# Group 1's coarse scores from unpooled q, a mask made later, and a replanned order

## The chip, the cores and the metric

The kernel runs on one core of a Trainium2 chip. The metric is device time in microseconds, the median over runs. The core has five engines with a queue each: TensorE (PE in the profile, its weight loads PEld), VectorE (DVE), ScalarE (ACT), GpSimd (POOL) and SyncE (SP), which here issues every DMA. An engine runs its instructions in the order in which they were written; engines wait for each other by semaphores.

## The reference, cut to what matters

Two attentions are added, and the sum goes through a dense layer pair. B = 8, H = 8, S = 576, D = 64; the dense part has 4608 tokens, width 512, inner width 2048.

```python
q_d = q.reshape(B, H, Sd, factor, D).mean(axis=3)      # factor 4, Sd = 144; k_d, v_d alike
out_d = sm_attn(q_d, k_d, v_d)                          # softmax attention, coarse
out_up = np.repeat(out_d, factor, axis=2)
mask = np.abs(pos[:, None] - pos[None, :]) < factor     # a band of 7
scores = np.where(mask, scale * np.matmul(q, k.transpose(0, 1, 3, 2)), -1000000000.0)
...
out_local = np.matmul(attn, v)
x = (out_up + out_local)        # to [B * S, H * D]
h = x @ w_in
g = h - np.tanh(h)
return (g @ w_out)
```

## The kernel before, in words

**Units.** Two heads of one batch make a pair p (0 to 31), two pairs a group n (0 to 15), four pairs a batch. A group's q and k (i = 0 for q, i = 1 for k) come in as fp32 tiles `qkn`; each of a group's pairs has an index y (0, 1).

**One group's preparation.** `reorder` (L480) casts to bf16 into `qr`. `turn` (L496) transposes with nine TensorE matmuls into a PSUM bank (L520), copies out to `qk` (L529, whole or a half per y), and pools by four with two adds: `half` (L533) and `qkd` (L538). Tables say which engine may do each of these: `RE` and `RS` for the cast (whole or halves), `TU` and `TS` for the copy, `AD` and `AS` for the adds. A table entry may leave the choice to the planner. `prep_v` casts v to `vw` (L443, table `CV`); `pool_v` pools v on TensorE with a constant (L462, L464) and copies it out to `vd` (L469, table `VD`).

**One pair's attention.** `s1` makes four of five blocks of the band's scores (L587); ACT takes the exponential (L623). `s2` makes the fifth block and the coarse scores (L606): for each half i of the pooled keys and each head hh one matmul of the pooled k with the pooled q, 144 columns wide; ACT takes two more exponentials (L649, L652). For the first four pairs the band's bias is added on TensorE (L581); for later ones DVE multiplies the exponentials by a 0/1 `mask` (L627, L656). `outs` multiplies with v (L669, L675); DVE takes the reciprocal of the sums (L686) and normalises into `ln` (L688). The result goes back into `xT`: for pairs in the table `UP` by matmuls that also repeat the coarse rows (L723, L728) and a copy on ACT or DVE (L734); else by transposes (L744 to L748) and an addition on DVE (L753); from pair 12 on by a DMA transpose and additions (L708).

**Banks.** Two PSUM banks `ps_ts` and two `ps_ox` serve all pairs; the first four have a second set, `ps_ts1` and `ps_ox1`, which is given to the dense part afterwards. Pairs that share a bank follow one another through it.

**Dense.** `mm1` (L777) makes 512 tokens by 128 inner columns, ACT takes the tanh (L786), DVE the difference into `gT` (L789); `mm2` (L832) makes the output, ACT copies it (L843), SP stores it. Block 0 needs the first batch's `xT`, that is pairs 0 to 3; block 1 needs pairs 4 to 7 too.

**Order.** Every piece of work is recorded with an engine (or alternatives), an assumed duration in ns, the keys it reads and writes, and a priority (10 per pair, 20 per group; lower is earlier). `Program.order` (L71) is a list scheduler: each engine takes the ready piece of the lowest priority at the planned time, with a fixed latency between engines (L25) and a margin `spare` (L254) which depends on the priority. The instructions are written out in the planned order, so the assumed durations set the order and not the time on the chip. `URG` raises the priority of chosen pieces (-2 is ahead of the dense part's -1); `LATE` sets the priority of a pair's output, normalisation and way back; `PLACE` and `PV` set where turns and pooled v stand among the pairs. Where the plan leaves TensorE idle early on, filler matmuls (L1064) are written.

**Constants.** POOL makes the identity, the group pattern, the bias, the repeating pattern `spread` (L313) and the mask (L317), which at L936 needs the bias alone and has priority 38.

Of the kernel before, what the change touches and what calls it, by code (L numbers as in the profile page):

```python
# [163 lines left out]
def kernel(  # L164
# [16 lines left out]
    G = S // 4  # L181
# [72 lines left out]
    def spare(pri, eng, to):  # L254
        if eng == "DMA":
            return 2500 if pri >= 140 else 1500 if pri >= 80 else 0
        level = (pri >= 120) + (pri >= LATER)
        return SPARE[to == "PE"].get(eng, (0, 0, 0))[level]
    LATER = 180
    SPARE = ({"POOL": (0, 500, 1000)},  # L260
             {"POOL": (0, 1000, 1500), "DVE": (0, 300, 800), "ACT": (0, 200, 500)})
    P.spare = spare
# [233 lines left out]
    def turn(n, i):  # L496
# [47 lines left out]
        for k, (ys, yy) in enumerate(each if parted else both):  # L544
            table = (TURN_H[parted - 1][k] if parted else
                     TURN[3 if n >= FI else TU.get((n, i), 1)])
            P.choice([(eng, ns, lambda fn=fn, ys=ys: copy(fn, ys)) for eng, ns, fn in table],
                     reads=ts, writes=[("qk", s, i, y) for y in yy],
                     pri=URG.get("turn", {}).get(n, pri))
        parted = AS.get((n, i), 0)  # L550
# [13 lines left out]
    def attention(p):  # L564
# [34 lines left out]
        def s2():  # L599
            for hh in range(2):  # L600
                score(4, hh, 512 * hh, sc2)
            for i in range(2):
                for hh in range(2):
                    rows = slice(64 * hh, 64 * hh + 64)
                    c = 512 * hh + 96 + G * i
                    T.matmul(sc2[:, c:c + G], pT[rows, 1, y, 16 * i:16 * i + 128],  # L606
                             pT[rows, 0, y, :], start=True, stop=True)
# [7 lines left out]
        qkds = [("qkd", sq, i, y) for i in range(2)]  # L615
# [10 lines left out]
        if not first:  # L626
            op("DVE", 900, lambda: V.tensor_tensor(  # L627
                out=e1, in0=e1,
                in1=mask[:, 0:480].unsqueeze(1).to_broadcast([128, 2, 480]),
                op=ALU.mult), reads=["mask"], writes=[("E", se, 0)], pri=pri)  # L630
# [4 lines left out]
        if MERGE <= p < NPAIR - 1:  # L635
            ahead, more = nexts[p + 1]

            def both():
                ahead()
                s2()  # L640
            op("PE", 800, both, reads=qks + qkds + more, writes=ts + ox, pri=pri)
        else:
            op("PE", 380 * cold, s2, reads=qks + qkds, writes=ox if p >= MERGE else ts,
               pri=pri)
# [10 lines left out]
        if not first:  # L655
            op("DVE", 450, lambda: V.tensor_tensor(  # L656
                out=e2v, in0=e2v,
                in1=mask[:, 480:576].unsqueeze(1).to_broadcast([128, 2, 96]),
                op=ALU.mult), reads=["mask"], writes=[("E", se, 1)], pri=pri)
# [191 lines left out]
    def dense(kb):  # L851
# [18 lines left out]
        if kb == NBLK:  # L870
# [5 lines left out]
    P_A, LATE = 5000, {0: 25, 2: 40, 3: 40}  # L876
# [5 lines left out]
    PV = {2: 0, 3: 0, 4: -1, 5: -1, 6: 0}  # L882
    PLACE = {2: (1, 3), 3: (1, 2), 4: (4, 4), 5: (1, 2), 6: (4, 4), 7: (1, 1), 8: (3, 3)}
# [7 lines left out]
    CV = {0: 3, 1: 0, 2: 0, 3: 3, 4: 0, 5: 0, 6: 3, 7: 1, 8: 2, 9: 0, 10: 1, 11: 3}  # L891
# [4 lines left out]
    RE = {(0, 0): 0, (0, 1): 0, (1, 0): 1, (1, 1): 1, (2, 0): 1, (2, 1): 0, (3, 0): 3, (3,  # L896
          1): 0, (4, 0): 2, (4, 1): 1, (5, 0): 0, (5, 1): 0}
# [3 lines left out]
    TU = {(0, 0): 0, (0, 1): 0, (1, 0): 2, (1, 1): 2, (2, 0): 0, (2, 1): 0, (3, 0): 2, (3,  # L901
          1): 0, (4, 0): 0, (4, 1): 1, (5, 0): 1, (5, 1): 0}
    re_v, re_a, re_p = (("DVE", 480, V.tensor_copy), ("ACT", 580, A.copy),
# [6 lines left out]
    VD = {0: 1, 1: 2, 2: 1, 3: 0, 4: 1, 5: 0, 6: 1}  # L910
    RS = {(0, 1): 2, (1, 0): 4, (1, 1): 1}
    UP = {0: 0, 1: 0, 2: 0, 3: 3, 4: 3, 8: 0, 11: 3}
    UP_COPY = [("ACT", 660, A.copy), ("DVE", 720, V.tensor_copy)]
    UP_H = [[("ACT", 370, A.copy)], [("DVE", 410, V.tensor_copy)]]
    half_v, half_p = ("DVE", 420, 260, V), ("POOL", 650, 500, GP)
# [5 lines left out]
    TS = {(0, 0): 1, (0, 1): 2, (1, 1): 2, (2, 1): 2, (4, 0): 2, (5, 0): 2, (5, 1): 1}  # L921
    AS = {(1, 0): 2, (1, 1): 1, (2, 0): 1, (2, 1): 1, (5, 0): 1, (5, 1): 4, (6, 1): 1}
    URG = {'e1': {4: -2, 5: -2, 6: -2, 7: -2, 8: -2, 9: -2, 10: -2, 11: -2}, 'e2': {0: -2,
          1: -2, 2: -2, 3: -2, 4: -2, 5: -2, 6: -2, 7: -2, 8: -2, 9: -2, 10: -2, 11: -2},
          'norm': {0: -2, 1: -2, 2: -2, 3: -2, 4: -2, 5: -2, 6: -2, 7: -2}, 'add': {0: -2,
          1: -2}, 'turn': {4: -2, 5: -2}, 'vd': {4: -2, 5: -2}}
    ADDERS = [[("DVE", 760, 440, V), ("POOL", 1190, 850, GP)],
              [("POOL", 1190, 880, GP)], [("DVE", 760, 440, V)]]
    AD = {(0, 0): 1, (0, 1): 0, (1, 0): 0, (1, 1): 1, (2, 0): 1, (2, 1): 0, (3, 0): 0, (3,
          1): 1, (4, 0): 0, (4, 1): 0, (5, 0): 0, (5, 1): 2}  # L930
# [28 lines left out]
    for p in range(NP):  # L959
        load_v(p)  # L960
    stages = []
# [134 lines left out]
```

The softmax here doesn't subtract the row's maximum and nothing guards it: scores larger than these inputs give would overflow.

## Time and profile before

| what | value |
|---|---|
| median of 6 runs | 335.49 us (334.8 to 336.36) |
| the profiled execution, whole | 334.8 us |
| its span, first to last instruction | 333.1 us |
| granted TensorE clock | 0.999 |
| PE busy | 319.6 us (96%) |
| PEld busy | 168.6 us (51%) |
| DVE busy | 234.9 us (71%) |
| ACT busy | 209.8 us (63%) |
| POOL busy | 155.1 us (47%) |
| mm1 and mm2 matmuls recorded | 553 and 540, 512 columns each |
| first dense matmul | 28.64 us |

A share of busy time is a mean over the whole span. The kernel has a front, in which the first four pairs are made, and a long stretch after it in which dense matmuls and the other 28 pairs share TensorE. Matmuls are pipelined: a row's duration is longer than the distance to the next one, so TensorE's work is read from distances between starts and from its idle time. A few matmul records are missing from the trace.

### The profile page before, as it was taken

How to read it: one execution, taken by the hardware profiler on the slowest of the kernel's cores; microseconds unless marked ns; L12 is line 12 of the kernel's file. 1: busy time of each engine (PE TensorE's matmuls, PEld its weight loads, DVE VectorE, ACT ScalarE, POOL GpSimd, SP SyncE). 2: the span in 40 equal slices, each digit the busy share in tenths (PEclk: the TensorE clock that was granted, in tenths of full speed). 3: DMA queues.
4: the chain of work that ended last, by engine and by line, in shares of the span. 5: the costliest groups of instructions: out<-in, count | busy, mean ns of one | idle time of the engine just before them, and what ended most of it. 6: DMA issues, size and time to landing. Idle time of an engine off the chain costs nothing.

```text
span 333.1 us, 6822 instructions
## 1 busy us (share of the span) xinstructions
PE 319.6 (96%) x2563; PEld 168.6 (51%) x2606; DVE 234.9 (71%) x386; ACT 209.8 (63%) x338; POOL 155.1 (47%) x183
## 2 busy tenths in 40 slices
PE   8778999999999999999999999999999999999996
PEld 5454555655554555554445444444444444444444
DVE  3698989689989879989688878787666443344300
ACT  1775877768958587667777786986654444434411
POOL 8673776249799479794938385752000000000000
PEclk9999999999999999999999999999999999999999
DMA  6999999998973899998999899742232100100012
GB/s 215 260 389 306 324 317 311 271 281 222 319 231 82 224 191 302 194 241 226 242 249 257 223 243 232 100 104 83 60 79 69 33 31 31 63 33 31 31 70 90
DMA packets 96878, 60.47 MB, mean 182 GB/s; under 512 B 74510, under 2 KB 80078, under 8 KB 96846
## 3 DMA queue, kind: packets, MB, share of 16 engines
q1 hardware_dynamic: 96846, 60.04, 67.1%
q8 instruction: 20, 0.33, 0.4%
q14 instruction: 12, 0.10, 0.1%
HBM read 43.05 MB, written 9.44 MB: 158 GB/s over the span
## 4 chain that ended last, share of the span: by engine, by line
PE 85%; DVE 6%; POOL 3%; issue 3%; ACT 1%; POOLq 0%; DVEq 0%; ACTq 0%
PE ps_hy L777 36%; PE ps_hy L832 34%; PE ps_ts L587 3%; PE ps_ox L669 3%; PE ps_ox L675 2%; PE ps_ts L520 2%; DVE ln L688 1%; DVE qk L529 1%; PE ps_hy L807 1%; DVE half L533 1%; ACT qk L529 1%; PE ps_ox L462 1%; POOL half L533 1%; PE ps_ox L606 1%; PE ps_ox L520 1%
## 5 line engine op out<-in xcount | busy, mean ns | idle before, releaser
L777 PE MATMUL ps_hy<-xT,w_in_sb 128*128 128x512 bf16 x553 | 141.8, 379 | 2.2 <-issue 1.1
L832 PE MATMUL ps_hy<-w_out_sb,gT 128*128 128x512 bf16 x540 | 137.2, 379 | 1.4 <-issue 0.5
L789 DVE TENSOR_TENSOR gT<-ps_hy,uy 128x512 bf16<-128x512 f32 x144 | 95.3, 685 | 56.7 <-ACT uy L786 55.3
L786 ACT ACTIVATE uy<-ps_hy 128x512 f32<-128x512 f32 x144 | 83.5, 601 | 61.9 <-PE ps_hy L777 57.2
L777 PEld LDWEIGHTS <-w_in_sb 128*128 128x128 bf16 x576 | 53.1, 98 | 59.3 <-issue 1.0
L832 PEld LDWEIGHTS <-gT 128*128 128x128 bf16 x560 | 52.3, 98 | 58.1
L533 POOL TENSOR_TENSOR half<-qk 128x576 f32<-128x576 bf16 (+1 forms) x33 | 34.8, 1058 | 44.9 <-ACT qk L529 39.7
L688 DVE TENSOR_TENSOR ln<-ps_ox,r 128x896 bf16<-128x896 f32 x30 | 32.7, 1089 | 0.8
L623 ACT ACTIVATE E<-ps_ts 128x960 bf16<-128x960 f32 x30 | 29.4, 980 | 2.1 <-PE ps_ts L587 2.1
L843 ACT COPY uy<-ps_hy 128x512 f32<-128x512 f32 x35 | 20.6, 590 | 14.3 <-PE ps_hy L832 12.6
L443 POOL CAST vw<-vst 128x640 bf16<-128x640 f32 x27 | 25.5, 949 | 7.6 <-DMA vst<-in_v_dram 4.1
L708 DVE TENSOR_TENSOR xT<-lnT 128x480 bf16<-128x480 bf16 (+1 forms) x40 | 27.8, 711 | 0.0
L627 DVE TENSOR_TENSOR E<-E,mask 128x960 bf16<-128x960 bf16 x28 | 23.5, 840 | 5.5 <-ACT E L623 5.5
L356 POOL TENSOR_TENSOR qkn<-qkn 128x512 f32<-128x512 f32 (+1 forms) x18 | 25.3, 1405 | 2.5 <-ACT uy L786 1.6
L529 ACT COPY qk<-ps_ts 128x1152 bf16<-128x1152 bf16 (+1 forms) x16 | 16.1, 1005 | 16.4 <-DVE qk L529 6.3
L538 POOL TENSOR_TENSOR qkd<-half 128x288 bf16<-128x288 f32 (+1 forms) x31 | 20.4, 661 | 5.8 <-DVE half L533 4.6
L529 ACT COPY qk<-vst 128x1152 bf16<-128x1152 bf16 x10 | 22.1, 2210 | 0.9 <-POOL half L533 0.7
L669 PEld LDWEIGHTS <-E 128*128 128x128 bf16 x300 | 15.3, 98 | 7.3 <-issue 0.6
L669 PE MATMUL ps_ox<-vw,E 128*128 128x65 bf16 x300 | 18.2, 194 | 0.5 <-DVE xT L734 0.3
L587 PEld LDWEIGHTS <-qk 64*128 64x128 bf16 x320 | 9.6, 95 | 17.9 <-issue 15.6
L491 POOL CAST qr<-qkn 128x1152 bf16<-128x1152 f32 (+1 forms) x14 | 16.1, 1156 | 4.8 <-DMA qkn<-in_k_dram 4.5
L491 DVE CAST qr<-qkn 128x1152 bf16<-128x1152 f32 (+1 forms) x18 | 16.4, 913 | 2.2 <-DMA qkn<-in_q_dram 2.2
(107 smaller groups left out, 294.6 us busy)
## 6 DMA issues: line engine op xcount, KB each, us to landing
vst<-in_v_dram SPq DMA_DIRECT2D x62, 160.0 KB, 4.8
qkn<-in_q_dram SPq DMA_DIRECT2D x32, 288.0 KB, 4.2
qkn<-in_k_dram SPq DMA_DIRECT2D x32, 288.0 KB, 4.9
out_dram<-uy SPq DMA_DIRECT2D x35, 256.0 KB, 2.4
qkn<-in_v_dram SPq DMA_DIRECT2D x9, 512.0 KB, 5.2
gT<-in_moe_w_in_dram SPq DMA_DIRECT2D x4, 1024.0 KB, 9.1
xT<-in_moe_w_out_dram SPq DMA_DIRECT2D x8, 256.0 KB, 4.4
gT<-in_moe_w_out_dram SPq DMA_DIRECT2D x2, 1024.0 KB, 8.9
```

The lines of the kernel that those rows point to most:

```text
L443: P.choice([(eng, ns, lambda fn=fn: fn(out=vw[w][:, 2 * jj:2 * jj + 2, :, 0:64], in_=vst[s])) for eng, ns, fn in CAST_V[CV.get(p, 1)]], re ...
L491: P.choice([(eng, ns, lambda fn=fn, x0=x0, x1=x1: fn(out=dst[:, x0:x1], in_=srt[:, x0:x1])) for eng, ns, fn in table], reads=[("qkn", sn, ...
L529: fn(out=o[:, ys].rearrange("p y (g a) -> p y g a", a=A6), in_=b16.rearrange("p (a g y) -> p y g a", a=A6, y=2)[:, ys])
L533: eng.tensor_tensor(out=half[:, ys], in0=four[:, ys, :, 0:2], in1=four[:, ys, :, 2:4], op=ALU.add)
L623: op("ACT", 980, lambda: A.activation(out=e1, in_=ps[:, :, 0:480], func=AF.Exp, scale=SCALE), reads=ts, writes=[("E", se, 0)], pri=URG.get ...
L669: T.matmul(po[:, hh, 65 * t:65 * t + 65], E[se][:, c:c + 128], vw[w][:, 2 * jj + hh, t, :], start=True, stop=True)
L688: op("DVE", 1090, lambda: V.tensor_tensor(out=ln[sl].rearrange("p n (h d) -> p h n d", d=D), in0=blocks[:, :, :, 0:64], in1=r[s].unsqueeze ...
L708: up=up: eng.tensor_tensor(out=xo[:, QW * t0:QW * t0 + nt * n].rearrange("p (t g a) -> p t g a", t=nt, a=4), in0=lnT[sl][:, t0:t0 + nt, 0: ...
L777: T.matmul(ps_hy[slot], w_in_sb[:, dc, fc * 128:(fc + 1) * 128], xT[dc][:, kb * 512:kb * 512 + 512], start=(dc == 0), stop=(dc == N_DC - 1))
L786: op("ACT", 490, lambda: A.activation(out=u[us], in_=ps_hy[slot], func=AF.Tanh), reads=[("hy", slot)], writes=[("u", us)], pri=-1)
L789: op("DVE", 620, lambda: V.tensor_tensor(out=gT[g][:, fc, :], in0=ps_hy[slot], in1=u[us], op=ALU.subtract), reads=[("hy", slot), ("u", us) ...
L832: T.matmul(ps_hy[slot], gT[g][:, fc, ts * 128:ts * 128 + 128], w_out_sb[:, fc, :], start=(fc == 0), stop=(fc == N_FF - 1))
```

## The change

Pairs of groups in the new set `QP` (group 1 alone) take their coarse scores from the unpooled q: the four tokens of a coarse row are read from `qk` with a step of four, in four matmuls that add up in PSUM. The pooled adds of that group's q (L533, L538) are left out. The mask is recorded after the loads of v, and waits for v of pair 1. Assumed durations and tables of the planner are set anew.

```diff
         level = (pri >= 120) + (pri >= LATER)
+        if 40 <= pri < 120 and to == "PE":
+            return MID.get(eng, 0)
         return SPARE[to == "PE"].get(eng, (0, 0, 0))[level]
-    LATER = 180
+    LATER = 200
...
+    MID = {'POOL': 0, 'DVE': 0, 'ACT': 0}
...
+        if i == 0 and n in QP:
+            return
         parted = AS.get((n, i), 0)
...
                     c = 512 * hh + 96 + G * i
+                    if hb in QP:
+                        for a in range(4):
+                            T.matmul(sc2[:, c:c + G], pT[rows, 1, y, 16 * i:16 * i + 128],
+                                     qT[rows, a:576:4], start=(a == 0), stop=(a == 3))
+                        continue
                     T.matmul(sc2[:, c:c + G], pT[rows, 1, y, 16 * i:16 * i + 128],
                              pT[rows, 0, y, :], start=True, stop=True)
...
-        qkds = [("qkd", sq, i, y) for i in range(2)]
+        qkds = [("qkd", sq, i, y) for i in range(hb in QP, 2)]
...
-            op("DVE", 900, lambda: V.tensor_tensor(
+            op("DVE", 780, lambda: V.tensor_tensor(
...
-            op("PE", 380 * cold, s2, reads=qks + qkds, writes=ox if p >= MERGE else ts,
+            op("PE", (380 + 400 * (hb in QP)) * cold, s2, reads=qks + qkds, writes=ox if p >= MERGE else ts,
...
-            op("DVE", 450, lambda: V.tensor_tensor(
+            op("DVE", 600, lambda: V.tensor_tensor(
...
-    P_A, LATE = 5000, {0: 25, 2: 40, 3: 40}
+    P_A, LATE = 5000, {1: 25}
...
-    PV = {2: 0, 3: 0, 4: -1, 5: -1, 6: 0}
-    PLACE = {2: (1, 3), 3: (1, 2), 4: (4, 4), 5: (1, 2), 6: (4, 4), 7: (1, 1), 8: (3, 3)}
+    PV = {2: -1, 3: 1, 4: 0, 5: -1, 6: 0}
+    PLACE = {2: (0, 0), 3: (0, 2), 4: (4, 4), 5: (1, 4), 6: (4, 4), 7: (1, 1), 8: (1, 3)}
...
-    CV = {0: 3, 1: 0, 2: 0, 3: 3, 4: 0, 5: 0, 6: 3, 7: 1, 8: 2, 9: 0, 10: 1, 11: 3}
+    CV = {0: 3, 1: 1, 2: 2, 3: 0, 4: 3, 5: 2, 6: 3, 7: 2, 8: 2, 9: 1, 10: 1, 11: 2}
...
-    RE = {(0, 0): 0, (0, 1): 0, (1, 0): 1, (1, 1): 1, (2, 0): 1, (2, 1): 0, (3, 0): 3, (3,
-          1): 0, (4, 0): 2, (4, 1): 1, (5, 0): 0, (5, 1): 0}
+    RE = {(0, 0): 0, (0, 1): 2, (1, 0): 0, (1, 1): 0, (2, 0): 1, (2, 1): 0, (3, 0): 3, (3,
+          1): 4, (4, 0): 2, (4, 1): 0, (5, 0): 0, (5, 1): 0}
...
-    TU = {(0, 0): 0, (0, 1): 0, (1, 0): 2, (1, 1): 2, (2, 0): 0, (2, 1): 0, (3, 0): 2, (3,
-          1): 0, (4, 0): 0, (4, 1): 1, (5, 0): 1, (5, 1): 0}
-    re_v, re_a, re_p = (("DVE", 480, V.tensor_copy), ("ACT", 580, A.copy),
+    TU = {(0, 0): 2, (0, 1): 1, (1, 0): 0, (1, 1): 2, (2, 0): 2, (2, 1): 0, (3, 0): 0, (3,
+          1): 1, (4, 0): 0, (4, 1): 0, (5, 0): 1, (5, 1): 0}
+    re_v, re_a, re_p = (("DVE", 640, V.tensor_copy), ("ACT", 620, A.copy),
...
-    VD = {0: 1, 1: 2, 2: 1, 3: 0, 4: 1, 5: 0, 6: 1}
-    RS = {(0, 1): 2, (1, 0): 4, (1, 1): 1}
-    UP = {0: 0, 1: 0, 2: 0, 3: 3, 4: 3, 8: 0, 11: 3}
+    VD = {0: 1, 1: 2, 2: 1, 3: 0, 4: 1, 5: 0, 6: 2}
+    RS = {(0, 1): 2, (1, 0): 1, (1, 1): 1, (2, 1): 1}
+    QP = {1}
+    UP = {0: 2, 1: 2, 2: 3, 3: 3, 4: 1, 8: 0, 11: 3}
...
-    half_v, half_p = ("DVE", 420, 260, V), ("POOL", 650, 500, GP)
+    half_v, half_p = ("DVE", 620, 420, V), ("POOL", 650, 500, GP)
...
-    TS = {(0, 0): 1, (0, 1): 2, (1, 1): 2, (2, 1): 2, (4, 0): 2, (5, 0): 2, (5, 1): 1}
-    AS = {(1, 0): 2, (1, 1): 1, (2, 0): 1, (2, 1): 1, (5, 0): 1, (5, 1): 4, (6, 1): 1}
-    URG = {'e1': {4: -2, 5: -2, 6: -2, 7: -2, 8: -2, 9: -2, 10: -2, 11: -2}, 'e2': {0: -2,
-          1: -2, 2: -2, 3: -2, 4: -2, 5: -2, 6: -2, 7: -2, 8: -2, 9: -2, 10: -2, 11: -2},
-          'norm': {0: -2, 1: -2, 2: -2, 3: -2, 4: -2, 5: -2, 6: -2, 7: -2}, 'add': {0: -2,
-          1: -2}, 'turn': {4: -2, 5: -2}, 'vd': {4: -2, 5: -2}}
-    ADDERS = [[("DVE", 760, 440, V), ("POOL", 1190, 850, GP)],
-              [("POOL", 1190, 880, GP)], [("DVE", 760, 440, V)]]
-    AD = {(0, 0): 1, (0, 1): 0, (1, 0): 0, (1, 1): 1, (2, 0): 1, (2, 1): 0, (3, 0): 0, (3,
-          1): 1, (4, 0): 0, (4, 1): 0, (5, 0): 0, (5, 1): 2}
+    TS = {(0, 0): 3, (0, 1): 3, (1, 1): 2, (2, 1): 1, (3, 0): 3, (4, 1): 2, (5, 0): 1}
+    AS = {(1, 0): 2, (1, 1): 2, (2, 0): 4, (2, 1): 4, (4, 0): 4, (5, 0): 1, (5, 1): 4, (6,
+          0): 1, (6, 1): 4}
+    URG = {'e1': {0: -2, 1: -2, 2: -2, 3: -2, 4: -2, 5: -2, 6: -2, 7: -2}, 'e2': {0: -2, 1:
+          -2, 2: -2, 3: -2, 4: -2, 5: -2, 6: -2, 7: -2}, 'od': {4: -2, 5: -2, 6: -2, 7: -2},
+          'add': {4: -2, 5: -2, 6: -2, 7: -2, 8: -2, 9: -2, 10: -2, 11: -2}, 'turn': {2: -2,
+          3: -2}}
+    ADDERS = [[("DVE", 850, 500, V), ("POOL", 1190, 850, GP)],
+              [("POOL", 1190, 880, GP)], [("DVE", 850, 500, V)]]
+    AD = {(0, 0): 1, (0, 1): 0, (1, 0): 0, (1, 1): 0, (2, 0): 1, (2, 1): 2, (3, 0): 1, (3,
+          1): 0, (4, 0): 0, (4, 1): 0, (5, 0): 0, (5, 1): 1}
...
-    op("POOL", 1660, c_mask, reads=["bias"], writes=["mask"], pri=38)
     if UP:
-        op("POOL", 2000, c_up, writes=["up"], pri=5)
+        op("POOL", 2300, c_up, writes=["up"], pri=5)
...
     for p in range(NP):
         load_v(p)
+    op("POOL", 1660, c_mask, reads=["bias", ("vst", 1, 1)], writes=["mask"], pri=38)
```

What the numbers in the tables mean, as far as they are used below: in `TS`, 2 is the first half on ACT and the second on DVE, 3 the other way round; in `AS`, 2 is the first half on DVE and the second on POOL, 4 both on POOL; in `CV`, 0 leaves POOL or ACT to the planner, 1 is POOL, 2 ACT, 3 DVE; in `UP`, 0 leaves ACT or DVE to the planner, 1 is ACT, 2 DVE, 3 the first half on ACT and the second on DVE; in `TU`, 0 leaves ACT or DVE to the planner, 1 is ACT, 2 DVE.

More of the change, by code (lines that the diff above doesn't have):

```diff
@@ L640, in both @@
                 s2()
-            op("PE", 800, both, reads=qks + qkds + more, writes=ts + ox, pri=pri)
+            op("PE", 800 + 400 * (hb in QP), both, reads=qks + qkds + more, writes=ts + ox, pri=pri)
         else:
-            op("PE", 380 * cold, s2, reads=qks + qkds, writes=ox if p >= MERGE else ts,
+            op("PE", (380 + 400 * (hb in QP)) * cold, s2, reads=qks + qkds, writes=ox if p >= MERGE else ts,
                pri=pri)
```

## The prediction

> **What bounds the kernel now.** I read the page first, then a table of short windows, then the chain that ended last in order of time, then each engine's timeline up to 76 us. The profiled execution took 334.8 us, the lowest of the runs shown (median 335.49); its span is 333.1, so 1.7 us lie around it. I make the sum against this execution and move the median by the same amount.
>
> The windows give start and end, length, then busy time of PE, PEld, DVE, ACT and POOL, then the clock and the DMA share:
>
> ```profile
> 10.00:15.00 5.00, 3.82 (x52) 2.46 (x50) 2.88 (x5) 3.33 (x6) 3.16 (x5) 1.00 1.07 228
> 15.00:20.00 5.00, 3.72 (x47) 2.32 (x47) 4.93 (x7) 3.74 (x8) 3.51 (x5) 1.00 1.02 346
> 20.00:25.00 5.00, 4.18 (x85) 3.44 (x84) 4.32 (x9) 4.29 (x9) 3.00 (x6) 1.00 1.05 388
> 25.00:30.00 5.00, 4.04 (x57) 2.58 (x54) 4.39 (x9) 1.76 (x4) 1.69 (x3) 1.00 1.06 379
> 30.00:35.00 5.00, 5.00 (x31) 2.55 (x30) 4.09 (x7) 3.88 (x7) 2.44 (x3) 1.00 0.99 243
> ```
>
> There are two stages. From 29.8 us on TensorE is full, at full clock. Before that it has holes, some of them padded with filler matmuls, and DVE is the nearly full engine from 15 us on. So a microsecond taken from DVE's path before 29.8 is worth a microsecond, while after 29.8 only TensorE's own work and its waits count. Those waits are few: summed over the trace after 29.8, TensorE waited visibly for another engine 0.9 us (0.44 at 99.96 for an xT copy, 0.29 at 53.06 for another, 0.17 at 138.06 for a mask product).
>
> The chain names what makes the front long (start, length, work):
>
> ```profile
> 8.51 1.64 POOL mask L317
> 10.15 1.12 POOL half L533
> 11.28 0.02 issue
> 11.30 0.65 ACT qk L529
> ...
> 16.67 0.83 DVE half L533
> 17.50 0.67 DVE qk L529
> 18.17 0.47 DVE qkd L538
> 18.64 0.02 issue
> 18.66 0.87 DVE half L533
> 19.54 0.02 issue
> 19.56 0.71 DVE qkd L538
> 20.27 0.05 issue
> 20.32 0.30 PE ps_ts L606 x4
> ```
>
> The mask stands on POOL ahead of group 0's first pooled add; then DVE carries the adds of group 1, and the scores of pair 2 (L606) wait for the last of them. Pair 0's output matmuls stand behind that on TensorE, so DVE's four normalisations start at 21.32 only. The last ends at 28.07; upsampling and copies take 1.7 us more, and dense work runs from 29.78.
>
> **Removed from DVE.** Group 1's q is no longer pooled. In the trace that is one half on DVE, 0.83 + 0.47 = 1.30 us of the chain, and one on POOL (0.78 + 0.42). For k, the second half's last add goes to POOL by the table: half of 0.71, so 0.35. The cast of v of pair 3 leaves DVE (0.48 busy); DVE then idled 0.44 for the outputs, but these come earlier too, so I count 0.45 (bounds 0 and 0.48). Together -2.1.
>
> **Added to DVE.** The xT copy of pair 0 is now DVE's alone; in the trace one whole copy ran on each of ACT and DVE. DVE's row is 0.76 with 0.67 to the next instruction: +0.7. Pair 2's copy is split, half of it on DVE (0.47 in the chain), after the last normalisation where little waits: +0.1 (0 to 0.47). The whole copy of group 1's q out of PSUM (1.35) may now go to ACT; which one the planner takes is not to be seen, so 0 (bounds -1.35 and 0; ACT was idle 0.88 us at 19.0).
>
> **The mask moves.** It is one instruction of 1.67 us and issues no DMA. On POOL it is moved past group 0's half add and qkd, past reorder casts and pair 1's v cast, to some time after v of pair 1 has landed. SP issues that load as the third of seven which take 5.97 us from 7.67, so by about 10.2; with landing times of 3.7 to 5.2 us that means 14 to 15.5. Ahead, POOL's half can start when ACT's copy is there (8.40 + 0.64) and not at 10.15. What is late next is the transposition on TensorE at 10.19, which ends at 10.86; ACT's copy at 11.30 follows it. I take 0.45 of the 1.1 us: -0.45 (bounds 0 and -1.1). Behind the moved mask stand k's half add and a v cast; the s2 of pair 2 waits for the first. POOL idled 3.17 us up to 16.41, waiting for a DVE copy, and this hole covers the mask. Without that cover it costs its 1.67. Its first user is pair 4's product at 39.86, far away.
>
> In its old place DVE was idle 2.95 us; in the new one DVE is full. The nearest rows are DVE's 288-element half adds: 0.92 at 16.58 beside a POOL add, 0.46 at 36.16, where DVE was first and POOL's took 0.94. So an overlap costs about 0.46; POOL's removed 1.2 us of group 1's q give some back. I take +0.3 (bounds -0.3 and 1.67).
>
> The Trainium skill ("SBUF — State Buffer", Who interferes with whom) speaks against the move: a DVE instruction with two SBUF inputs and a GpSimd instruction that reads SBUF exclude each other, and the later one blocks until the first is done. These two rows agree. Taken at its worst that page would make this term +1.67 and the whole sum -0.1.
>
> **Added to TensorE.** In s2 of pairs 2 and 3 each coarse score matmul becomes four. Now there are four coarse matmuls per pair (two halves by two heads, 144 columns each); then there are 16, so 12 more per pair, 24 in all. The rows:
>
> ```profile
> 20.32 0.30 PE L606 MATMUL ps_ts<-qkd 64*128 64x144 bf16 x4 [0.28 <-DVE qkd L538]
> 20.55 0.33 PE L669 MATMUL ps_ox<-vw,E 128*128 128x65 bf16 x5
> 13.61 0.68 PE L520 MATMUL ps_ox<-ident,qr 128*128 128x128 bf16 x9
> ```
>
> No row reads its moving operand with a step of four. The L520 transposes, each with new weights on the same rows, follow each other every 56 ns for 128 columns, so 144 take 63 ns: 16 x 63 = 1.0 us against 0.12 for the present four, +0.9 per pair, 1.8 in all. A bound from above is a matmul by its full duration, 223 ns each (3.6 us per pair); below, pairs of them overlapping as the four do now (0.5 us). It is added where TensorE has holes (1.28 us idle between 15 and 20), and the outputs of pair 3 come 2.7 us after its s2 at 21.91. That slack hides it; without it 1.8 us would count. I take +0.2 (bounds 0 and 1.8, twice what the upper bound of 3.6 leaves beyond the slack of 2.7).
>
> The Trainium skill ("TensorE: Matmul & The Clock Gate", The mechanism) states that weight loads overlap running matmuls only where the row group differs. The four matmuls of one head share their rows, so each would pay its load of 98 ns too: 24 x 161 = 3.9 us in place of 1.5. The L669 row differs: five matmuls on the same rows in 0.16 us, so the loads of 98 ns are hidden there, and I go by the row.
>
> Front: -2.1 + 0.7 + 0.1 - 0.45 + 0.3 + 0.2 = -1.25 us.
>
> **Replanned.** LATE lets pair 0's output go first and pair 1's later; this fills DVE's holes and is in the -2.1. MID gives zeros, as SPARE did for these priorities: nothing. LATER takes margin from pairs 18 and 19; pairs 12 to 17 have the smaller margin now and show only the wait of 0.17: +0.1 (0 to 0.5). Adds of group 2 go wholly to POOL, four halves of 0.67 + 0.42: 4.4 us against DVE and POOL together until 39.94. Pair 4's output comes at 48.6 only, so nothing. Pair 4's xT copy whole on ACT (0.64) in place of two halves one after the other takes away the wait at 53.06: -0.3. Sum -1.45.
>
> **The rivals.** (A) The gain is caught at the first block boundary. The second block's mm1 needs pair 7's xT:
>
> ```profile
> 68.95 0.74 DVE L753 TENSOR_TENSOR xT<-ps_ox,od 128x576 bf16<-128x576 bf16 x1
> 69.47 1.03 PE L777 MATMUL ps_hy<-xT,w_in_sb 128*128 128x512 bf16 x4
> ```
>
> There is no slack: the add ends at 69.69 and its user (the last two of the four) starts at 69.9. If dense work starts 1.25 us earlier and pairs 4 to 7 do not, TensorE runs dry for 1.25 and about 335.2 is left. For it: the DMA share is about 1.0 throughout, so group 3's q and k land no earlier. Against it: group 3's q copy waited on DVE from 44.4 to 46.5 and is urgent now, which pulls the following outputs of pair 4 (48.6) forward by up to 2 us.
>
> (B) Slower: the normalisations lose their urgent rank, in the same stretch. Pairs 4 to 7 go one after the other through one pair of banks, and each 1.09 us normalisation could stand behind a subtraction, mask or cast of 0.65 to 0.93: four times 0.8 is 3.2 us on that series. Less the 2 us from the copies, xT of pair 7 is 1.2 us later than now, while TensorE is out of other work 1.25 earlier: 2.45 us idle, so 335.49 - 1.45 + 2.45 = 336.5, and to 338 with the mask's 1.67. It is slower from the point where that xT ends beyond about 71 us. Against it: their rank is still ahead of later pairs.
>
> (C) The step of four reads at a fraction of the speed, or the mask blocks DVE as above: the front gains nothing, 335.3. (D) ACT takes the whole copy, a further 1.35 off: 332.6.
>
> **How the numbers follow.** Forecast 0.50, A 0.15, B 0.20, C 0.08, D 0.07. The time is the forecast's, 335.49 - 1.45 = 334.0, its own range 332.8 to 335.0. The range for all is 332.0 (D with the start's other 0.6) to 337.0 (B's first part). A difference of 0.3% (1.0 us) is about what this measurement can tell from no change. Faster by over that: most of the forecast and D, 0.54; within: 0.19; slower: B and a little of C, 0.27.
>
> **What would show it.** Right: the first dense matmul row at 28 to 29 us; no POOL mask ahead of half; about 16 L606-type matmuls in 1.0 us for pairs 2 and 3; TensorE without a hole near 68. Wrong: a hole of over 1 us before the second block, DVE rows of 0.9 where 0.46 stood, or a front that ends after 29.5.

## The result and the profile after

The changed kernel takes 336.47 us (median of 22 runs, 335.57 to 337.6); the kernel before, run beside it, 335.37 us (47 runs). The ratio is 1.0033, with a 95% interval of 1.0023 to 1.0042: 1.1 us slower, where 1.45 us faster was forecast. The profiled execution took 337.27 us, its span is 335.5.

The first view is the table of short windows of the changed kernel, with the columns that it had for the kernel before:

```profile
15.00:20.00 5.00, 4.55 (x65) 2.88 (x63) 4.29 (x7) 4.80 (x9) 1.58 (x2) 1.00 1.01 343
20.00:25.00 5.00, 5.00 (x93) 4.12 (x88) 3.35 (x6) 3.92 (x9) 4.69 (x8) 1.00 1.05 387
25.00:30.00 5.00, 4.05 (x64) 2.76 (x62) 4.11 (x7) 2.06 (x5) 1.78 (x3) 1.00 1.06 379
30.00:35.00 5.00, 4.88 (x29) 2.45 (x29) 4.07 (x8) 3.60 (x7) 0.67 (x1) 1.00 1.02 252
```

DVE (third busy time) fell from 4.93 to 4.29 between 15 and 20 us and from 4.32 to 3.35 in the next window. TensorE (first) rose from 3.72 to 4.55 and from 4.18 to 5.00. This execution starts its transposes 1.12 us later than the profiled one of before (see the table below). Windows moved by as much (16.12 to 21.12 and 21.12 to 26.12 us) give DVE 3.17 and 4.46 and TensorE 5.00 and 4.70, so the reading holds over the two windows together: DVE's work did leave, and TensorE became the busier engine. The chain of waits of that stretch, in order of time (start, length, work), says the same:

```profile
19.78 1.04 PE ps_ts L613 x16
20.82 0.27 PE ps_ox L679 x5
...
21.59 0.26 DVE r L696
```

Pair 2's 16 coarse matmuls (L613) stand on TensorE ahead of pair 0's outputs (L679), and DVE's first reciprocal waits for these. DVE's timeline shows the wait, in the bracket at the end of the row:

```profile
21.59 0.25 DVE L696 RECIPROCAL r<-ps_ox 128x14 f32<-128x14 f32 x1 [2.27 <-PE ps_ox L685]
```

DVE idles 2.27 us here; before it idled 0.44. The copy of pooled v that the outputs also need had been ready at 19.54, 1.2 us before they started.

The second loss is behind the front. This is the timeline of all engines from 45 us on:

```profile
46.05 0.76 DVE L532 COPY qk<-ps_ox 128x576 bf16<-128x576 bf16 x1 [1.04 <-ACT qk L532]
...
46.95 1.15 POOL L536 TENSOR_TENSOR half<-qk 128x576 f32<-128x576 bf16 x1 [2.14 <-DVE qk L532]
...
48.13 1.12 ACT L532 COPY qk<-ps_ts 128x1152 bf16<-128x1152 bf16 x1 [2.12 <-POOL half L536]
...
49.31 0.39 PE L592 MATMUL ps_ts<-qk 64*128 64x120 bf16 x8 [0.86 <-ACT qk L532]
```

The brackets make a chain. DVE's half of group 3's q copy waits for ACT's half; POOL's add waits for DVE; ACT's copy of group 3's k waits for POOL's add, from which it takes no data; pair 5's scores wait for ACT. TensorE stands still for 0.86 us, in a stretch in which the kernel before has no visible wait of over 0.44. Behind the front, TensorE's visible waits for other engines (those over 0.12 us) add up to 1.83 us here and to 0.90 us in before. In the plan the add and the k copy started 2 ns apart, the add first, so it is the first in the written order.

To compare runs I use three numbers from each profile. The **start** is the first row of the transposes on TensorE (6.91 us before). The **front** goes from there to the end of the last xT copy of pairs 0 to 3. The **rest** goes from there to the end of the span.

| kernel | median us (runs) | ratio to before, 95% interval | start | first reciprocal after it | front | rest |
|---|---|---|---|---|---|---|
| before | 335.37 (47) | 1 | 6.91 | 14.41 | 22.82 | 303.36 |
| before_again | 335.38 (12) | 0.9992 [0.9975, 1.0008] | 7.86 | 13.82 | 22.22 | 303.32 |
| after | 336.47 (22) | 1.0033 [1.0023, 1.0042] | 8.03 | 13.56 | 22.59 | 304.83 |
| again | 337.40 (6) | 1.0058 [1.0041, 1.0075] | 7.57 | 13.18 | 22.22 | 306.03 |
| one_of_four | 336.02 (12) | 1.0022 [1.0009, 1.0036] | 7.97 | 12.80 | 21.84 | 306.20 |
| outs_first | 338.39 (6) | 1.0082 [1.0061, 1.0102] | 7.92 | 12.09 | 23.01 | 306.00 |
| copy_ahead | 336.57 (7) | 1.0033 [1.0017, 1.0050] | 6.43 | 13.51 | 23.28 | 305.30 |
| q_alone | 335.16 (12) | 0.9985 [0.9966, 1.0004] | 7.87 | 13.09 | 21.70 | 303.75 |
| q_outs | 335.41 (12) | 0.9993 [0.9973, 1.0014] | 7.49 | 11.95 | 21.75 | 304.72 |
| replan_alone | 338.41 (6) | 1.0081 [1.0057, 1.0104] | 7.16 | 13.96 | 22.76 | 306.87 |
| mask_late | 335.25 (12) | 0.9998 [0.9982, 1.0013] | 6.55 | 14.22 | 22.62 | 304.51 |
| q_mask | 334.88 (12) | 0.9988 [0.9973, 1.0002] | 7.15 | 13.08 | 21.69 | 303.77 |
| tables_back | 336.35 (12) | 1.0039 [1.0016, 1.0062] | 7.84 | 13.18 | 22.21 | 305.62 |
| times_back | 335.39 (12) | 1.0013 [0.9996, 1.0030] | 7.15 | 13.19 | 22.23 | 303.39 |
| times_copy | 335.33 (12) | 1.0006 [0.9992, 1.0020] | 6.96 | 13.18 | 22.96 | 304.87 |
| q_mask_one | 335.41 (12) | 0.9995 [0.9971, 1.0018] | 7.00 | 12.30 | 21.46 | 304.59 |
| best_a | 334.75 (11) | 0.9979 [0.9951, 1.0006] | 6.97 | 13.08 | 21.44 | 304.82 |
| best_b | 334.77 (12) | 0.9980 [0.9959, 1.0001] | 7.43 | 13.08 | 21.39 | 303.41 |
| best_b_again | 334.64 (12) | 0.9970 [0.9951, 0.9988] | 6.49 | 13.09 | 21.42 | 304.42 |

Two things must be known to read it. The start is not the change's doing: the same kernel has it at 6.91 and at 7.86. So 1.12 us of the 2.4 by which the two profiled spans differ (8.03 - 6.91) is chance; front (-0.23) and rest (+1.47) hold what is left. And the rest of one execution can be a microsecond off that of the next (304.83 in `after` and 306.03 in `again`, the same kernel), so times are judged by the medians. Even these move between sessions, which ran on different chips: the changed kernel came to 1.0033 in one and to 1.0058 in another, 0.8 us apart. The ratio is to before's runs in the same session.

Of the signs that the prediction named, those of the edits came: no mask ahead of the half add, 16 matmuls in 1.13 us, no hole near 68 us. A sign of being wrong came too: the front ends at 30.6 us, and the first dense matmul stands at 29.81. Of that lateness 1.12 us is the start.

### The profile page after: what moved, and what is told of

Read it like the earlier page. It is cut to its first block, busy times and chain, and to the rows that moved or that the text cites. A ratio compares the mean times of both kernels' runs of the same rounds, so it can differ in the third digit from the quotient of the medians.

```text
span 335.5 us, 6872 instructions
## 1 busy us (share of the span) xinstructions
PE 323.4 (96%) x2589; PEld 170.6 (51%) x2631; DVE 230.6 (69%) x378; ACT 211.8 (63%) x340; POOL 153.3 (46%) x190
## 4 chain that ended last, share of the span: by engine, by line
PE 77%; DVE 10%; ACT 3%; issue 3%; DMA 2%; SPq 2%; POOL 1%; ACTq 0%; DVEq 0%; POOLq 0%
PE ps_hy L842 32%; PE ps_hy L787 31%; PE ps_ts L592 3%; DVE gT L799 3%; PE ps_ox L679 2%; DVE ln L698 2%; ACT qk L532 2%; PE ps_ox L685 2%; PE ps_ts L523 2%; DMA qkn<-in_k_dram 1%; DVE E L637 1%; SPq L409 1%; PE ps_ox L465 1%; PE ps_hy L817 1%; ACT uy L796 1%
## 5 line engine op out<-in xcount | busy, mean ns | idle before, releaser
L536 POOL TENSOR_TENSOR half<-qk 128x576 f32<-128x576 bf16 (+1 forms) x36 | 36.2, 1012 | 50.4 <-ACT qk L532 36.4
L637 DVE TENSOR_TENSOR E<-E,mask 128x960 bf16<-128x960 bf16 x28 | 25.5, 910 | 7.9 <-ACT E L633 7.7
L718 DVE TENSOR_TENSOR xT<-lnT 128x480 bf16<-128x480 bf16 (+1 forms) x40 | 25.6, 658 | 0.0
L359 POOL TENSOR_TENSOR qkn<-qkn 128x512 f32<-128x512 f32 (+1 forms) x18 | 23.9, 1329 | 2.7 <-DVE E L666 1.5
L541 POOL TENSOR_TENSOR qkd<-half 128x288 bf16<-128x288 f32 (+1 forms) x36 | 23.2, 650 | 1.0
L446 POOL CAST vw<-vst 128x640 bf16<-128x640 f32 x24 | 19.4, 809 | 5.5 <-DMA vst<-in_v_dram 5.4
L494 POOL CAST qr<-qkn 128x1152 bf16<-128x1152 f32 (+1 forms) x14 | 14.9, 1070 | 11.8 <-DMA qkn<-in_k_dram 11.6
L679 PEld LDWEIGHTS <-E 128*128 128x128 bf16 x300 | 15.2, 98 | 7.0 <-issue 0.7
L679 PE MATMUL ps_ox<-vw,E 128*128 128x65 bf16 x300 | 18.0, 194 | 0.4 <-DVE qk L532 0.2
L494 DVE CAST qr<-qkn 128x1152 bf16<-128x1152 f32 (+1 forms) x17 | 15.3, 899 | 3.1 <-DMA qkn<-in_q_dram 3.0
```

The lines of the kernel that those rows point to most:

```text
L494: P.choice([(eng, ns, lambda fn=fn, x0=x0, x1=x1: fn(out=dst[:, x0:x1], in_=srt[:, x0:x1])) for eng, ns, fn in table], reads=[("qkn", sn, ...
L536: eng.tensor_tensor(out=half[:, ys], in0=four[:, ys, :, 0:2], in1=four[:, ys, :, 2:4], op=ALU.add)
L637: op("DVE", 780, lambda: V.tensor_tensor(out=e1, in0=e1, in1=mask[:, 0:480].unsqueeze(1).to_broadcast([128, 2, 480]), op=ALU.mult), reads= ...
L679: T.matmul(po[:, hh, 65 * t:65 * t + 65], E[se][:, c:c + 128], vw[w][:, 2 * jj + hh, t, :], start=True, stop=True)
L718: up=up: eng.tensor_tensor(out=xo[:, QW * t0:QW * t0 + nt * n].rearrange("p (t g a) -> p t g a", t=nt, a=4), in0=lnT[sl][:, t0:t0 + nt, 0: ...
```

## The experiments

**The changed kernel and three edits of it.** `again` is the changed kernel unchanged. `one_of_four` and `copy_ahead` differ from it in one thing, `outs_first` in two moves. For moves, pieces of work are named as they are recorded, and the planned list is rearranged before it is written out (`whole` is the way back by repeating matmuls, `up` its copy into `xT`).

```diff
 one_of_four:
-                        for a in range(4):
-                            T.matmul(..., qT[rows, a:576:4], start=(a == 0), stop=(a == 3))
+                        T.matmul(..., qT[rows, 0:576:4], start=True, stop=True)
 outs_first:
+    move outs(0), outs(1) ahead of the bias of s2(2); mm of pool_v(1) ahead of whole(0)
 copy_ahead:
+    move copy(3, k) ahead of half(3, q)
```

> The changed kernel once more, as the base of the other three. Its profiled execution began 1.1 us late: q's second half landed at 5.7 us and DVE's first cast took 1.48 us beside a POOL select, against 4.9 us and 0.77 us in the kernel before. If that start is chance, this profile may show either start, and the time stays near 336.5. If the change causes it, the cast begins at 5.7 to 5.8 us again. Measured from the end of that cast, the changed front should be the same 0.2 us shorter than that of before.

> Leaves out three of the four q matmuls of each coarse score of group 1 (only the first of four tokens counts), in the same order, so the two groups of 16 matmuls shrink from 1.1 us to 0.3 each. Theory, TensorE's queue holds the front (pair 0's outputs wait behind pair 2's 16 matmuls): the first reciprocal comes 0.85 us earlier and the time falls by 0.7 to 1.1 us. Rival, DVE holds the front and TensorE's slack hides the matmuls: the time stays within 0.2 us.

> Nothing is left out: on TensorE the outputs of pairs 0 and 1 go ahead of pair 2's coarse scores, and the pooling of v for pairs 2 and 3 ahead of pair 0's upsampling; everything else keeps its place. Theory, TensorE's queue: the first reciprocal starts 1.0 us earlier relative to the first cast, the front ends 0.5 to 1.0 us earlier and the time falls by as much. Rival, DVE holds the front: no gain, DVE only idles elsewhere.

> One ACT instruction, the copy of group 3's k, is written ahead of POOL's half add of group 3's q (they are planned 2 ns apart), so it no longer waits for that add. Theory, this wait is most of what the dense stretch lost: the 0.9 us hole before pair 5's first scores near 49 us goes, and the time falls by 0.7 to 1.0 us. Rival, the hole is filled by later waits (the second block starts at the same moment because pair 7 sets it): the hole goes but the time stays within 0.2 us.

`again` starts its transposes at 7.57 us, where the same kernel had 8.03; `copy_ahead`, which differs behind the front alone, has 6.43. So the late start was chance.

With one matmul of four (the scores of pairs 2 and 3 then come from one token in four) the time falls from 1.0058 to 1.0022, and DVE's wait from 2.25 to 1.48 us: in this order and session the extra matmuls cost about 1.2 us (0.0036 of 335). Against the 1.0033 of `after` it would be 0.4. The front is only 0.4 us shorter than that of `again`, so where the rest of the 1.2 lies is not shown. Writing the outputs first did not get that back, it cost: 1.0082. With it I had moved pooled v of pair 2 ahead of pair 0's way back, DVE's copy of it then stood behind a wait of 1.78 us, and the third reciprocal came later, at 26.61 instead of 26.31. With the k copy ahead of the add the hole at 49 us is gone and the ratio is 1.0033 against 1.0058 in the same session; the intervals overlap slightly.

**One part alone, in the written order of before.** Here nothing is replanned. Pieces are dropped or moved in the old list, so every other instruction keeps its place.

```diff
 q_alone:
+                    if hb == 1:
+                        for a in range(4):
+                            T.matmul(sc2[:, c:c + G], pT[rows, 1, y, 16 * i:16 * i + 128],
+                                     qT[rows, a:576:4], start=(a == 0), stop=(a == 3))
+                        continue
+    leave out half(1, q) and qkd(1, q)
 q_outs, besides:
+    move outs(1), outs(0) ahead of the bias of s2(2)
 mask_late:
+    move the mask behind the second half(1, k) on POOL
 q_mask:
+    both q_alone and mask_late
 q_mask_one: q_mask, with one matmul of four as in one_of_four
```

> The kernel before, unchanged: a second profile of it, to say which of its numbers repeat. All theories: ratio 1.000 (within 0.1%). If the loss of the changed kernel sits in the dense stretch because of its order, the excess spacing of TensorE's matmuls after xT of pairs 0 to 3 is done stays near this kernel's 10.6 us here too (9.8 to 11.4), with no hole at 49 us; if that number jitters by itself as it does between the two profiles of the changed kernel (11.6 and 12.7), it reaches 12 or more here, and the dense stretch proves nothing.

> The kernel before in its own written order; only the pooled adds of group 1's q are left out and pairs 2 and 3 take four matmuls for each coarse one. Mask, tables and all else as before. Theory (the replanned order lost the time, and the burst of 16 matmuls takes back about half of what DVE saves): the first reciprocal 0.5 to 0.9 us earlier than before's 21.32 at the same start, the dense stretch as before, 334.8 us or ratio 0.998 (0.996 to 0.999). Rival 1 (the 24 extra matmuls count in full on TensorE and the four-part scores are the loss): 1.8 more on TensorE, ratio 1.001 to 1.003. Rival 2 (the burst is hidden as the prediction had it, -1.30 + 0.2): ratio 0.9965 or lower.

> As q_alone, and on TensorE the outputs of pairs 1 and 0 stand ahead of pair 2's fifth block and coarse scores. Theory (TensorE's order hides DVE's saving): outputs start when vd of pair 0 is there, some 18.8 us, the first reciprocal at 19.5 to 20.0 where before has 21.32, and the time is 1.0 to 1.6 us under before, ratio 0.9955 to 0.997. Rival (later links of the front, pooled v of pair 2 or the exponentials of pairs 2 and 3, end last anyway): no better than q_alone. Rival of the block boundary: front earlier by 1 us or more in the profile, and the time no better than q_alone.

> The kernel before in its own written order; the mask alone moves, on POOL from ahead of group 0's first pooled add to behind POOL's half add of the second half of group 1's k. Nothing else. Theory (the mask's 1.66 us on POOL held group 0's add up by 1.1 us, and of that about half reaches the end of the front): the first reciprocal 0.3 to 0.6 us earlier than before at the same start, the dense stretch 303.3 to 303.8 us, ratio 0.9985 (0.997 to 1.000). Rival 1 (in the new place it holds up DVE's adds and casts or v of pair 2 behind it on POOL, and so the pooled v of pair 2): the front no shorter or up to 1 us longer, ratio 1.000 to 1.003. Rival 2 (DVE, and not POOL, sets the front, so the early gain is waited away): ratio 1.000 (0.999 to 1.001).

> The change without its replanning: the kernel before in its own written order with q of group 1 unpooled as in q_alone, and the mask moved as in mask_late. Theory (both edits gain, and the replanned tables lose): ratio 0.997 (0.9955 to 0.9985), about 334.4 us, with the dense stretch within 0.5 us of 303.4. Rival (the two gains are the same wait, on which TensorE's 16 matmuls and the outputs behind them end last): no better than q_alone, 0.9985. Rival of the weights' arrival: the front shorter by another 0.4 us or more, and a hole of as much near 53 to 58 us where mm2 waits for w_out.

> As q_mask, but each coarse score of pairs 2 and 3 takes only the first of its four matmuls (scores of these pairs from one token in four, so the output differs). It prices the 24 extra matmuls in the order of before, where nothing else is moved. Theory (TensorE runs in order and has no slack between pair 2's scores and pair 1's outputs, so the extra matmuls count): pair 2's coarse matmuls take 0.3 us where q_mask has 1.2, the first reciprocal 0.6 to 0.9 us earlier than q_mask's, the front 0.5 to 1.0 us shorter, ratio 0.995 to 0.9975 against before. Rival (the prediction's: a slack hides them): as q_mask, 0.9988, front within 0.2 us of it.

`before_again` repeats the rest of `before` to 0.04 us, with the same holes: these two executions of the order of before do not lose what the new one loses.

`q_alone` has its start at 7.87, as `before_again` (7.86), so the two can be laid side by side: first reciprocal 0.73 us earlier, front 0.52 shorter, rest 0.43 longer. Its time is 0.9985, with an interval that includes 1. This is its timeline:

```profile
19.05 1.20 PE L622 MATMUL ps_ts<-qk,qkd 64*128 64x144 bf16 x16
...
20.96 0.25 DVE L705 RECIPROCAL r<-ps_ox 128x14 f32<-128x14 f32 x1 [1.06 <-PE ps_ox L694]
```

The burst of 16 takes 1.14 us to the next row's start, and DVE waits 1.06 us behind it. With one matmul of four (`q_mask_one`) that wait is 0.32, and the reciprocal comes 0.78 us earlier still (13.08 to 12.30 after the start). But the time does not follow: 0.9995 against 0.9988. The timeline of `q_mask_one` tells why:

```profile
19.30 0.24 DVE L706 RECIPROCAL r<-ps_ox 128x14 f32<-128x14 f32 x1 [0.32 <-PE ps_ox L695]
...
26.93 1.18 DVE L448 CAST w_in_sb<-gT 128x512 bf16<-128x512 f32 x2 [0.89 <-DMA gT<-in_moe_w_in_dram]
...
28.52 0.81 PE L800 MATMUL ps_hy<-xT,w_in_sb 128*128 128x512 bf16 x3 [1.09 <-DVE xT L757]
```

DVE is done with its normalisations at 26.0 and then stands at a cast of w_in whose data land at 26.9. Pair 3's xT copy is written behind that cast, so mm1 waits 1.09 us. Here my expectation fell: the matmuls do count for DVE, but the front is only 0.23 us shorter than that of `q_mask` (21.46 and 21.69), because a load that did not come earlier with the front takes most of it back.

In `q_outs` (0.9993) the first reciprocal is 1.14 us ahead of `q_alone`'s and the front no shorter either, but for another reason. Both bursts now stand ahead of the pooled v of pairs 2 and 3, and DVE waits for that:

```profile
23.30 0.69 DVE L483 CAST vd<-ps_ts 128x512 bf16<-128x512 f32 x1 [1.23 <-PE ps_ts L478]
```

So the third reciprocal comes no earlier after the start (17.44, and 17.39 in `q_alone`). Behind the front, mm2 is held for 1.25 us at 57.9 us by a cast of w_out, whose data land at 56.9.

`mask_late` gains nothing (0.9998). From the start to the transposes of group 1's q it is 6.70 us in `before`, and 6.34 to 6.36 in `before_again`, `mask_late`, `q_mask` and `after`. The old mask ends at 10.0 to 10.2 us in `before`, `before_again`, `q_alone`, `q_outs` and `replan_alone`, whose transposes start at 6.91 to 7.87; it is in the way only where TensorE starts early. What the move then wins meets a load, as POOL's timeline of `mask_late` shows:

```profile
12.08 0.67 POOL L505 CAST qr<-qkn 128x576 bf16<-128x576 f32 x1 [0.81 <-DMA qkn<-in_k_dram]
```

POOL waits 0.81 us for group 1's k. In its new place the mask took 2.17 us and DVE's two adds beside it 0.87 (0.92 before): it was POOL that was stretched and not DVE, whose adds came later (19.06 us, the mask 18.68). So the blocking of DVE that the prediction weighed for this place did not come. With both edits (`q_mask`) the time is 0.9988, no better than `q_alone`'s 0.9985.

**The replanning alone, and its parts.** `replan_alone` is the changed kernel with q of group 1 pooled and the mask in its old place. `tables_back` and `times_back` take the changed kernel and set one of its two kinds of planner input back. `times_copy` is `times_back` with the k copy moved as in `copy_ahead`.

```diff
 replan_alone:
-    QP = {1}
+    QP = set()
 (and the mask's line back at its old place)
 tables_back:
-    LATER = 200
+    LATER = 180
 (PV, PLACE; CV, UP, URG from pair 4 on; TU, TS, AS, AD, RE, RS, VD from group 2 on: as before)
 times_back:
-    re_v, re_a, re_p = (("DVE", 640, V.tensor_copy), ("ACT", 620, A.copy),
+    re_v, re_a, re_p = (("DVE", 480, V.tensor_copy), ("ACT", 580, A.copy),
-    half_v, half_p = ("DVE", 620, 420, V), ("POOL", 650, 500, GP)
+    half_v, half_p = ("DVE", 420, 260, V), ("POOL", 650, 500, GP)
 (ADDERS, the two mask products and c_up likewise)
```

> The changed kernel with q of group 1 pooled again and the mask made where it was before, replanned with the new tables and assumed times. Theory (the new tables and times lose by themselves, in the dense stretch): 336.0 to 337.5, ratio 1.002 to 1.006, with holes of 0.3 us and more between 46 and 53 us as in the changed kernel. Rival 1 (the four-part scores or the mask are the loss): ratio 1.000 or lower. Rival 2 (the new tables only pay with q unpooled, since DVE and POOL have 2.5 us more to do in the front): ratio above 1.006, the loss in the front.

> The changed kernel, with the planner's tables for groups from 2 and pairs from 4 on, their urgent ranks, places and LATER set to those of before; the tables of the front, the four-part scores, the mask's place and all assumed times stay as changed. Theory 1 (the later tables lose): most of the loss in the dense stretch goes, no hole at 49 us, dense 303.3 to 304.3 us, time 334.5 to 335.7, ratio 0.998 to 1.001. Theory 2 (the longer assumed times make the planner write another order, whatever the tables): the dense stretch stays at 304.8 or more, ratio 1.002 or more. Theory 3 (an order planned for other assumed times is a lottery): holes at other places, 304.3 to 306.

> The changed kernel, with the assumed times of DVE and POOL set back to those of before; all tables stay as changed. Theory 1 (the later tables lose): as the changed kernel or worse, ratio 1.003 to 1.008, dense stretch over 304.8. Theory 2 (the assumed times lose): dense 303.3 to 304.3 us, ratio 0.998 to 1.001. Theory 3 (lottery): holes at other places than in the changed kernel, 304.3 to 307.

> As times_back (the changed kernel with the assumed times of before), and ACT's copy of group 3's k written ahead of POOL's half add of group 3's q. Theory (the hole of 1.03 us ahead of pair 5's scores is the k copy behind the add, and what is then left is the changed kernel without its loss): the hole near 48 us under 0.3, dense stretch 302.4 to 303.0, ratio 0.998 to 1.0000. Rival (another wait takes its place within the next 10 us): a new hole of 0.5 us or more between 50 and 60, dense 303.2 to 304.5, ratio as times_back's 1.0013 or above.

`replan_alone` is, with `outs_first`, the slowest of all, 1.0081 or 2.7 us. Its front is as long as before's (22.76), its rest 3.5 us longer. TensorE's longest waits after 30 us, from the view of waits (what waited, for what; us in total, times, longest):

```profile
PE ps_hy L787 <- DVE gT L799: 1.6, 3, 1.1
PE ps_ts L592 <- ACT qk L532: 0.9, 1, 0.9
...
PE ps_ox L679 <- ACT qk L532: 0.6, 1, 0.6
```

They lie at 47, 49, 142, 167 and 176 us: dense work waiting for a subtraction on DVE, scores for a copy, outputs for a copy. `tables_back` has no hole at 49 us but others (0.29 at 72.8, 0.39 at 105.0, 0.87 at 167.6) and is no faster, 1.0039; `q_mask` beside it in that session has 0.9988. `times_back` keeps the 0.87 us wait for the k copy, has no later hole in its profile, and comes to 1.0013. With the k copy moved as well (`times_copy`) it is 1.0006, 335.33 us, the time of before. Its profiled execution, at 336.5 us above its own median, shows other waits:

```profile
52.70 0.20 PE L693 MATMUL ps_ox<-vw,E 128*128 128x65 bf16 x1 [0.79 <-DVE E L680]
...
58.34 1.02 PE L859 MATMUL ps_hy<-w_out_sb,gT 128*128 128x512 bf16 x4 [1.04 <-POOL w_out_sb L451]
```

So the replanned order loses, and its waits lie at places that change with each replanning. No part of the input is shown to be the loss by itself. Setting the later tables back shows no gain (1.0039). Setting the assumed times back takes off 0.7 us against `after` (1.0033 to 1.0013, intervals that overlap) and 1.5 against `again` (1.0058). The k copy takes off 0.2 us (1.0013 to 1.0006) or 0.8 (1.0058 to 1.0033), with overlapping intervals both times. What is then left, 1.0006, can't be told from before.

**A version that beats both.** `best_a` is `q_mask` with the xT copies of pairs 3 and 4 whole on ACT; their two halves, planned side by side, ran one after the other (0.40 and 0.46 us against 0.64 for a whole copy). `best_b` also gives ACT two copies of DVE's.

```diff
 best_a:
+    up(3), up(4): one whole copy on ACT, no halves
 best_b, besides:
+    up(0) and vd of group 1: ACT in place of DVE; vd behind the last exponential of pair 3
+    move outs(2) ahead of whole(0)
```

> As q_mask, and the xT copies of pairs 3 and 4, which were two halves on two engines one after the other (0.40 and 0.46 us), are one whole copy on ACT (0.64). Theory: the front 0.15 to 0.3 us shorter, the hole of 0.45 us near 52 us at 0.25 or less, together 0.3 to 0.5 us under q_mask, ratio 0.9972 to 0.998 against before. Rival (TensorE catches up the gain at the arrival of w_out or at the next block): within 0.1% of q_mask's 0.9988.

> As best_a, and ACT instead of DVE takes the copy of the pooled v of group 1 and the xT copy of pair 0 (ACT idles 1.6 us at either), and pair 2's outputs are written ahead of pair 0's way back. Theory (DVE is the nearly full engine between the first reciprocal and the end of the front, with 8.6 us of work there, and loses 1.45 of it): the third reciprocal 0.4 to 0.7 us earlier than in q_mask at the same start, ratio 0.9955 to 0.997. Rival (w_in's last slices or w_out end last): front shorter, time no better than best_a.

> The kernel of best_b unchanged, on another chip, because its interval against before, 0.9959 to 1.0001, just reaches 1. Theory (it beats both kernels): ratio 0.9965 to 0.999, and the dense stretch within 0.6 us of 303.4 in a second profile. Rival (its gain was the noise of one chip): 0.9995 to 1.001, with a hole of over 0.7 us somewhere after the front.

`best_b_again` is 0.9970 with an interval of 0.9951 to 0.9988: 1.0 us under before and some 2 us under the changed kernel. Of the versions in the order of before it is the only one whose interval leaves out 1. The step from `best_a` to `best_b` isn't shown to gain: beside each other they are 0.9979 and 0.9980, where 0.9955 to 0.997 was expected. And the second profile has a rest of 304.42 with a wait of 1.20 us for w_out at 56.3 us, which was the rival's sign. DVE's timeline of `best_b` shows the next limit:

```profile
24.59 0.24 DVE L707 RECIPROCAL r<-ps_ts 128x14 f32<-128x14 f32 x1 [1.43 <-PE ps_ts L696]
```

DVE now idles 1.43 us before the third reciprocal, for outputs that wait for pooled v, which stands behind the second burst of 16. The third reciprocal is only 0.23 us earlier than in `q_mask` (17.16 and 17.39 after the start), where 0.4 to 0.7 was expected.

## Why the prediction was wrong

**The step that failed** is "Replanned": LATER "+0.1", group 2's adds "so nothing", pair 4's copy "-0.3". All the new tables and assumed times were priced at -0.2 us together, because the work that they move lies beside a full TensorE. The assumed durations, PLACE, PV and the split copy of group 3's q have no term at all. (MID is rightly "nothing", and the wait for pair 4's copy at 53.06 did go.) The runs show +1.5 us: q_mask, which has both edits in the old order, is at 0.9988, the changed kernel at 1.0033, and 0.0045 of 335.4 is 1.5; with the 1.0058 of `again` it is 2.3. Alone the replanning costs 2.7. The reasoning asked which durations changed and not what the new list puts ahead of what. In `after`, two pieces planned 2 ns apart became a wait of 2.12 us for ACT and of 0.86 us for TensorE, which, at 96%, has no slack behind the front to take it. That wait is only part of the loss: TensorE's visible waits explain 0.9 of the 1.5 us by which the rest grew in `after` (1.95 of 2.7 in `again`), and what the remainder is stays open.

**The front** was forecast at -1.25 us. In the changed kernel next to nothing of that is left: 22.59 and 22.22 us, against 22.82 and 22.22 in the two profiles of before. In the old order the two edits shorten it (`q_mask`, 21.69) by 1.1 us against the profile that the sum was made from, which started nearly as early, and by 0.5 against the other. Their time gains 0.4 us, in an interval that includes none. In the new order they are worth more, 1.6 us (1.0081 to 1.0033) with 0.2 of it in the front, or by `again` 0.8 (to 1.0058) with 0.5 in the front.

- DVE's lost work, -1.30 for group 1's q: about right. Without most of the burst (`q_mask_one` against `before_again`) the first reciprocal comes 1.52 us earlier (13.82 to 12.30).
- The other 0.8 us taken from DVE (half of a k add, a v cast) was worth nothing: DVE was done with its last add at 19.33 and idled until 21.59.
- The 24 matmuls, "+0.2, that slack hides it": the size of a burst was right (+0.9: 1.13 us for 16, where the four of before take 0.22 and not the 0.12 of the sum), the slack was looked up at the wrong pair. Pair 3's outputs have 2.7 us, but the burst of pair 2 stands ahead of the outputs of pairs 0 and 1. It costs 0.78 at the first reciprocal; in the time 0.4 to 1.2 us in the new order, and nothing that shows in the old one (0.9988 and 0.9995).
- The mask, -0.45 + 0.3: measured 0.0 in the time, with 0.36 where TensorE starts early and none where it starts late.
- The copy of pair 0 on DVE, +0.7: from first to third reciprocal it is 4.72 in the changed kernel and 4.31 in q_mask, so +0.4.
- What no term held: casts of w_in and w_out wait for loads, which land at 26.9 us in `q_mask_one` and at 54 to 57 us, and which a shorter front does not bring forward. Where they end last, they take back what the front gained.

**The rivals.** B named 336.5 us, and that is the time, but by luck, for its mechanism did not happen: pair 7's xT is done at 70.7, where B decides from 71, and mm1 of the second block starts at 72.68 without a wait for it. A did not bind either. D did not come: DVE took the whole copy (1.34 us at 15.86). C's step of four did not decide it: in the burst a matmul comes to 71 ns, against 63 assumed. It isn't free, though: four coarse matmuls take 0.35 us to the next row's start with the step (`q_mask_one`), and 0.22 to 0.23 without it (`before`).

The weight-load rule that the prediction weighed ("TensorE: Matmul & The Clock Gate", The mechanism, in the Trainium skill), that loads overlap matmuls only where the row group differs, is not borne out by this case. The 16 loads, four in a row on the same 64 rows and 92 to 113 ns each, lie hidden in 1.13 us of matmuls. Paid in full, 16 x (63 + 112), they would make 2.8; even with the two halves of the rows side by side, 1.4. The same section also allows a load into a background weight buffer, which would fit.

## What to carry to other kernels

Price a replanned order by what it puts ahead of what, not by the durations that moved: run the functional edit in the old order first, and the replanning alone. Before a slack is credited, look who stands behind the new work on its own in-order engine, not who uses its result. And before a front is shortened, find the loads that will not come earlier with it: here a first reciprocal 0.8 us earlier gave nothing.

## What was not expected of the hardware

- The first 29 filler matmuls take 5.93 us in one execution and 6.88 in another of the same kernel: 266 ns from one to the next at first, 136 later, and the change comes after 14 of them or after 21. The transposes behind them start at 6.91 or 7.86. The Trainium skill says that the number of slow matmuls at the start varies from run to run ("TensorE: Matmul & The Clock Gate", Part 1: The HAM clock gate); these rows agree.
- SP issued the last w_out loads of the first half at 40.72 us in `before`, 41.06 in `before_again`, 42.60 in `again` and 43.03 in `after`, behind a v load whose issue took 2.44 us in the first and 3.65 in the last. In `again`, `times_copy`, `q_outs` and `best_b_again` mm2 then waited 0.7 to 1.25 us for w_out; in the two profiles of before it did not, nor in `after`, which issued them late. What sets this lateness wasn't settled: `replan_alone`, one of the two slowest kernels, issued them at 39.93, ahead of all four of these.
